# A gated mix of linear attention and a gated MLP: block products for half of the down projection, stored weights, and scaled tokens

## The chip, the core and the metric

The kernel runs on one core of a Trainium2 chip. The metric is the device time of one execution in microseconds (us); lower is better. The engines are named as in the profile: PE is the matrix engine (PEld its weight loads), DVE the vector engine, ACT the scalar engine, POOL the GpSimd engine, and SP the engine that only issues the DMAs here. Matrix products read SBUF and write PSUM, which has eight banks of 128 rows by 512 columns of f32.

## The reference

```python
S, D, H, F = 2048, 576, 32, 4608          # tokens, model width, heads, hidden width
g = sigmoid((x * gate_w).sum(-1, keepdims=True))     # one gate per token
a = linear_attention(x, wqkv, w_phi) @ wo            # softmax feature maps, 32 heads of 18
gate, up = x @ W_gate, x @ W_up                      # [S, F] each
h = gate * (gate > 0) * up
b = h @ W_down                                       # [S, D]
out = g * a + (1 - g) * b
```

Everything is f32. The kernel gets near f32 precision from products in fp32r: each operand is split into a high part (its rounding to fp32r, made by ACT as a copy) and a low part (what is left, made by DVE as a subtraction), and each product is three matmuls, high by high, high by low and low by high.

## The kernel before

All arrays are kept transposed: features lie on the partitions, tokens on the free axis, 512 tokens to a block.

**Attention, first part** (to about 260 us in the profile): keys, values and queries of the 16 blocks of 128 tokens, one after another (loop over `t`). POOL multiplies half of each softmax. The gate's logit is a column of the values' product; `gate_logits` (L258) turns it into exp(-logit), and after the loop two small DVE instructions make g.

**Attention, second part** (to about 417 us): for each block of 512 tokens `sums`, `invert`, `divide` and `project_out`. g * a goes to the DRAM buffer `att` (L557). `gates` (L504, L505) spreads 1-g of each token over all 128 partitions, into `ngb`. The operands of the MLP are made in the same stretch by `x_operands` (L564 loads, L569 to L571 split, four subtractions on DVE between them).

**MLP** (the rest): `units` are the 2 halves of the tokens times 36 chunks of 128 hidden features. For gate and up the kernel multiplies 2x2 blocks (features halved by tokens halved) with 7 products instead of 8: `product(ps, u, n)` (L720) is product `n` of unit `u`, 7 matmuls of 128x128 by 128x512 each. Its weights are split in each unit anew, in both halves of the tokens: `load_w` (L601) brings 768 KB, `split_blocks` makes the operand tile `wb`, `split_sums` four sums of blocks (L621 to L624) and the operand tile `ws` (L604 on ACT, L607 and L608 on DVE). The seven operands `xo` of the tokens are exchanged between the halves, in the last unit of the first half (`prep`, from `x_operands(1)`).

The hidden blocks are split into `hh` and `hl`. The down projection runs one group of two chunks behind, in pieces between the products, for each row block `m` of the output and token block `t`:

```python
            for u in us:
                hh, hl = HID[u, t]
                w = WD[u][:, m * P:(m + 1) * P]
                pairs += [(w, hh), (w, hl)]
                if m < 4:
                    pairs.append((WD[u][:, DK + m * P:DK + (m + 1) * P], hh))
```

That is 8 x 6 matmuls for the four full row blocks and 2 x 4 for the fifth, which carries the high and the low part of its 64 rows side by side: 56 for a group of two units, with 2 x 49 of the products beside them. Two of the ten sums stay in PSUM over the whole half (`pm`); the other eight are added to `ac` in SBUF by DVE after each group (L770). After the last group of a half, `finish` loads `att` (L733), multiplies by `ngb` (L740), adds (L741) and stores (L742), for each of the ten blocks.

The order on each engine comes from a planner that goes by priorities in program order, except inside `in_order`, which pins the order as written on DVE, ACT and SP for the early operands. Buffers are rings: a tile waits until its predecessor in the ring has been read.

Of the kernel before, what the change touches and what calls it, by code (L numbers as in the profile page):

```python
# [47 lines left out]
@contextmanager  # L48
def in_order(tc, nc):

    traced = nc.cur_bb.bb.instructions
    last = {i.engine: i for i in traced}
    n = len(traced)
    yield
    for i in traced[n:]:
        if i.engine in (nc.vector.engine, nc.scalar.engine, nc.sync.engine):
# [6 lines left out]
def gated_mix_kernel(  # L63
# [33 lines left out]
    ngb = keep.tile([P, S], F32, name="ngb")  # L97
# [3 lines left out]
    gs = keep.tile([P, 4 * NT], F32, name="gs")[:, :NT]  # L101
# [158 lines left out]

    def queries(t):
# [81 lines left out]

    for t in range(2, NT - 1):
        if t in (6, 10):
            load_x(t // 4 + 1)
        if t == 12:
            AR.close()
# [44 lines left out]
    nc.vector.tensor_scalar_add(gs, gs, 1.0)  # L393
    nc.vector.reciprocal(gs, gs)
# [56 lines left out]
    rx = ctx.enter_context(tc.tile_pool(name="rx", bufs=1, **L_))  # L451
# [107 lines left out]

    def x_operands(hf):  # L560

        def load(k, t, slot):
            a = rx.tile([P, 3, TB], F32, name=f"xr{slot}")
            nc.sync.dma_start(a, xs[:, k, :, (2 * hf + t) * TB:(2 * hf + t + 1) * TB])  # L564
            return a

        def operand(name, a):
            o = (xo2 if name in (3, 4) else xo).tile([P, 5, TB], F32R, name="xo", tag="xo")
            nc.scalar.activation(o[:, 0:3], a, AF.Copy)  # L569
            tt(out=o[:, 3:5], in0=a[:, 0:2], in1=o[:, 0:2].bitcast(F32), op=SUB)  # L570
            tt(out=o[32:64, 2], in0=a[32:64, 2], in1=o[32:64, 2].bitcast(F32), op=SUB)  # L571
            XO[hf, name] = o

        b11, b12, b22 = load(0, 0, 0), load(0, 1, 1), load(1, 1, 2)
        operand(1, b11)
        yield
        tt(out=b11, in0=b12, in1=b11, op=SUB)
        operand(5, b11)
        yield
        tt(out=b11, in0=b22, in1=b11, op=SUB)  # L580
        operand(6, b11)
        yield
        tt(out=b12, in0=b22, in1=b12, op=SUB)
        operand(7, b12)
        b21 = load(1, 0, 1)
        yield
        operand(2, b21)
        yield
        operand(3, b22)
        yield  # L590
        tt(out=b21, in0=b21, in1=b11, op=SUB)
        operand(4, b21)
        yield
# [4 lines left out]
    def load_w(u):  # L598
        if u < len(units):
# [3 lines left out]
    def split_w(o, a, after=None):  # L603
        i = nc.scalar.activation(o[:, :, 0:3], a, AF.Copy)  # L604
        if after:
            tc.add_manual_dep(i.ins, after.ins.name, NO_SYNC, reason="after")
        tt(out=o[:, :, 3:5], in0=a[:, :, 0:2], in1=o[:, :, 0:2].bitcast(F32), op=SUB)  # L607
        tt(out=o[64:96, :, 2], in0=a[64:96, :, 2], in1=o[64:96, :, 2].bitcast(F32), op=SUB)  # L608

    def split_blocks(u, after=None):  # L610

        if u < len(units):
            o = wop.tile([P, 3, 5, P], F32R, name="wb")
            split_w(o, RAW[u][:, 0:3], after)
            WO[u] = {1: (o, 0), 2: (o, 1), 4: (o, 2)}

    def split_sums(u):

        if u < len(units):
            a = RAW.pop(u)  # L620
            tt(out=a[:, 2], in0=a[:, 2], in1=a[:, 3], op=ADD)  # L621
            tt(out=a[:, 3], in0=a[:, 0], in1=a[:, 3], op=SUB)
            tt(out=a[:, 0], in0=a[:, 2], in1=a[:, 0], op=SUB)
            tt(out=a[:, 1], in0=a[:, 1], in1=a[:, 0], op=SUB)  # L624
            o = wop.tile([P, 4, 5, P], F32R, name="ws")
            split_w(o, a)
            WO[u].update({5: (o, 2), 6: (o, 0), 7: (o, 3), 3: (o, 1)})

# [4 lines left out]
    early = x_operands(0)  # L633

    def later():
        with in_order(tc, nc):
            next(early)

    behind = iter(())
    for n, tb in enumerate(order):  # L640
# [50 lines left out]
    wdp = ctx.enter_context(tc.tile_pool(name="wdp", reuse_waits="tile", bufs=2))  # L691
    hp = ctx.enter_context(tc.tile_pool(name="hp", reuse_waits="tile", bufs=7))
    tp = ctx.enter_context(tc.tile_pool(name="tp", reuse_waits="tile", bufs=5))
    ac = ctx.enter_context(tc.tile_pool(name="ac", reuse_waits="tile", bufs=1))
    px = ctx.enter_context(tc.tile_pool(name="px", bufs=2, space=PSUM, reuse_waits="tile"))
# [81 lines left out]
    def step():  # L777
        next(behind, None)
# [142 lines left out]
```

## Time and profile before

| What | Value |
|---|---|
| Median of 3 runs | 1705.72 us (1703.13 to 1708.34) |
| The profiled execution | 1707.41 us |
| Its span in the profile | 1705.6 us |
| Granted PE clock, mean | 0.98 |
| PE busy | 1648.6 us, 7834 matmuls |
| DVE, ACT, POOL busy | 1291.1, 624.0 and 46.0 us |
| DMA | 128.48 MB, mean 75 GB/s |

The span is what the profile records from the first to the last instruction; the execution's own time has 1.8 us around it. A matmul's record ends later than the next one starts, since they are pipelined, so how many start in a stretch says more than how long each is. A row of a table by stretches gives the stretch, its length, then for each engine the busy time and the number of instructions (x), then the granted clock, the share of time in which the 16 DMA engines were busy, and GB/s.

### The profile page before, as it was taken

The numbers are of one execution on the slowest core, as the hardware profiler recorded it, in microseconds if no ns is written. First come the engines' busy times: TensorE is split into PE (matmuls) and PEld (weight loads), VectorE is DVE, ScalarE is ACT, GpSimd is POOL, SyncE is SP. The second block draws the span as 40 slices with busy tenths as digits, with TensorE's granted clock in tenths as the row PEclk, the third lists the DMA queues.
The fourth block names the chain that finished last, engine by engine and source line by source line (L and its number), as shares of the span: only waits on it lengthen the run. The fifth ranks groups of instructions, "written<-read, shape, count | busy, mean of one in ns | idle before, by whom it ended". The sixth has DMA issues, their size and how long they took to land.

```text
span 1705.6 us, 19899 instructions
## 1 busy us (share of the span) xinstructions
PE 1648.6 (97%) x7834; PEld 1379.0 (81%) x7834; DVE 1291.1 (76%) x1966; ACT 624.0 (37%) x895; POOL 46.0 (3%) x53
## 2 busy tenths in 40 slices
PE   9999997988999999999999998999999999999996
PEld 8899995666888888888888886788888888888885
DVE  5877675666778777777778779977777777777776
ACT  4233335554533333333323334433333332333330
POOL 0121210000000000000000000000000000000000
PEclk9899997889999999999999999999999999999998
DMA  5211113535221211122122212421111222121203
GB/s 182 69 37 58 44 44 96 170 127 169 83 70 65 70 51 60 61 65 70 51 70 66 70 51 70 149 83 62 63 61 52 70 65 70 51 70 60 63 18 105
DMA packets 42329, 128.48 MB, mean 75 GB/s; under 512 B 4906, under 2 KB 5546, under 8 KB 42236
## 3 DMA queue, kind: packets, MB, share of 16 engines
q1 hardware_dynamic: 42236, 127.22, 23.1%
q8 instruction: 61, 1.00, 0.2%
q14 instruction: 32, 0.26, 0.0%
HBM read 108.50 MB, written 16.74 MB: 73 GB/s over the span
## 4 chain that ended last, share of the span: by engine, by line
PE 86%; DVE 5%; DMA 4%; ACT 2%; issue 1%; SPq 1%; DVEq 0%; ACTq 0%
PE cx L720 26%; PE pd L763 19%; PE ca L720 13%; PE cy L720 6%; PE pm L763 5%; PE pq L150 4%; PE pk L150 3%; PE pv L150 3%; PE kv L319 2%; PE pwo L150 2%; PE ptr L283 1%; DMA ga<-att 1%; PE po L150 1%; DMA xr<-xs 1%; DMA wdr<-wd 1%
## 5 line engine op out<-in xcount | busy, mean ns | idle before, releaser
L763 PE MATMUL pd<-hh,wd 128*128 128x512 f32 x1008 | 357.5, 390 | 2.2 <-DVE ac L770 2.2
L720 PE MATMUL cx<-xo,ws 128*128 128x512 f32 x1008 | 253.2, 390 | 5.3 <-DVE ws L608 2.2
L720 PE MATMUL cx<-xo,wb 128*128 128x512 f32 x1008 | 252.5, 390 | 2.8 <-DVE o L556 1.4
L720 PE MATMUL ca<-xo,ws 128*128 128x512 f32 x1008 | 253.4, 390 | 0.8 <-DVE ws L608 0.6
L720 PEld LDWEIGHTS cx<-xo,ws 128*128 128x128 f32 x1008 | 188.8, 188 | 46.6 <-ACT g L789 2.7
L763 PE MATMUL pd<-hl,wd 128*128 128x512 f32 x576 | 224.6, 390 | 0.0
L720 PEld LDWEIGHTS cx<-xo,wb 128*128 128x128 f32 x1008 | 188.9, 188 | 43.8 <-DVE o L556 1.9
L763 PEld LDWEIGHTS pd<-hh,wd 128*128 128x128 f32 x1008 | 189.4, 188 | 43.1 <-DVE ac L770 3.5
L720 PEld LDWEIGHTS ca<-xo,ws 128*128 128x128 f32 x1008 | 189.2, 188 | 42.2 <-ACT wd L708 1.0
L770 DVE TENSOR_TENSOR ac<-pd,ac 128x512 f32<-128x512 f32 x272 | 187.5, 690 | 33.1 <-PE pd L763 33.1
L123 ACT ACTIVATE hh<-g 128x512 fp32r<-128x512 f32 x144 | 83.0, 621 | 294.3 <-DVE g L822 294.3
L708 ACT ACTIVATE wd<-wdr 128x576 fp32r<-128x576 f32 x72 | 48.8, 679 | 262.2 <-PE pd L763 256.0
L604 ACT ACTIVATE ws<-wr 128x1536 fp32r<-128x1536 f32 x72 | 107.3, 1490 | 59.5 <-DVE wr L624 59.5
L720 PE MATMUL cy<-xo,wb 128*128 128x512 f32 x504 | 126.6, 389 | 0.0
L763 PEld LDWEIGHTS pd<-hl,wd 128*128 128x128 f32 x576 | 108.4, 188 | 22.4
L607 DVE TENSOR_TENSOR ws<-wr,ws 128x1024 fp32r<-128x1024 f32 x72 | 88.2, 1225 | 44.1 <-ACT ws L604 43.9
L607 DVE TENSOR_TENSOR wb<-wr,wb 128x768 fp32r<-128x768 f32 x72 | 69.0, 958 | 55.1 <-ACT wb L604 53.5
L720 PEld LDWEIGHTS cy<-xo,wb 128*128 128x128 f32 x504 | 94.6, 188 | 19.6
L763 PE MATMUL pm<-hh,wd 128*128 128x512 f32 x288 | 101.0, 389 | 0.0
L800 ACT ACTIVATE g<-cx 128x512 f32<-128x512 f32 x72 | 43.1, 598 | 153.4 <-PE cx L720 147.4
L822 DVE SCALAR_TENSOR_TENSOR g<-g,cx 128x512 f32<-128x512 f32 x72 | 49.5, 687 | 60.2 <-PE cx L720 60.1
L815 DVE TENSOR_TENSOR g<-ca,g 128x512 f32<-128x512 f32 x72 | 49.8, 691 | 58.4 <-PE ca L720 58.3
(180 smaller groups left out, 2555.2 us busy)
## 6 DMA issues: line engine op xcount, KB each, us to landing
wr<-wgu SPq DMA_DIRECT2D x72, 768.0 KB
wdr<-wd SPq DMA_DIRECT2D x72, 288.0 KB
eT<-et SPq DMA_DIRECT2D x12, 594.0 KB
er<-eT SPq DMA_DIRECT2D x12, 594.0 KB
xr<-xs SPq DMA_DIRECT2D x8, 768.0 KB
att<-o SPq DMA_DIRECT2D x16, 256.0 KB
ga<-att SPq DMA_DIRECT2D x16, 256.0 KB
outT<-o SPq DMA_DIRECT2D x16, 256.0 KB
```

Of the source, the lines that this page charges most:

```text
L123: nc.scalar.activation(hi, src, AF.Copy)
L150: nc.tensor.matmul(ps, w, m, start=i == 0, stop=i == len(pairs) - 1)
L319: nc.tensor.matmul(kv[j // 2][:vn + 1, j % 2, :gn], v[:, j * GS:j * GS + vn + 1], flat(e)[:, c0:c0 + gn], start=False, stop=t == NT - 1, s ...
L604: i = nc.scalar.activation(o[:, :, 0:3], a, AF.Copy)
L607: tt(out=o[:, :, 3:5], in0=a[:, :, 0:2], in1=o[:, :, 0:2].bitcast(F32), op=SUB)
L708: nc.scalar.activation(o[:, :D], w, AF.Copy)
L720: nc.tensor.matmul(ps, w, v, start=first and m == 0, stop=m == len(pairs) - 1, skip_group_check=True)
L763: nc.tensor.matmul(ps, w, v, start=i == 0 and (g == 0 or not perm), stop=i == len(pairs) - 1 and (g == NGR - 1 or not perm))
L770: tt(out=ACC[m, t], in0=ps, in1=ACC[m, t], op=ADD)
L800: nc.scalar.activation(g2, cx, AF.Copy)
L815: tt(out=g2, in0=ca, in1=g2, op=ADD)
L822: nc.vector.scalar_tensor_tensor(out=g, in0=g, scalar=0.0, in1=up, op0=ALU.max, op1=MULT)
```

## The change

1. **Down projection, second half of the tokens**: each group of two chunks is treated as 2x2 blocks (two hidden chunks by two 128-row blocks of the output, with two token blocks) and multiplied with 7 products of 3 matmuls instead of 8 (`down`). The fifth row block still takes 8 matmuls, of the hidden blocks 1, 5, 2 and 4 of the seven. The hidden operands are seven sums instead of four blocks; the sums of weights are made by POOL (`down_sums_of_blocks`). The first half keeps its 56 matmuls a group (`down_plain`). The pieces are now one to a product, in `slot`: piece j of seven follows product j of the unit, in the order 1, 5, 6, 3, 7, 2, 4 of the block products, and DVE's addition of a piece is queued behind the product after it. Pieces 1, 6, 7, 4 add up in one PSUM bank, the others use a second.
2. **Gate and up weights**: the split operand tiles `wb` and `ws` of the first half are stored in DRAM (`wbd`, `wsd`, 0.98 and 1.31 MB a unit) and loaded in the second half instead of being made again (`load_operands`). In the first half unit u makes the weights of unit v = u + 1 (`make`). The units 0 and 1 are split before the MLP begins.
3. **Tokens times the root of 1-g**: the MLP's tokens are scaled beforehand, so that the hidden values carry 1-g and `finish` is gone: `ac` starts as `att`, loaded at the beginning of a half, and is stored as it is. The root needs g of half of the tokens early (`half_gates`, with an ACT square root), spread over the partitions (`on_all_rows`); POOL scales the tokens and makes the differences (`scaled_sums`), in the attention's first part for the first half and during the MLP's first half for the second. The seven operands go to DRAM (`xt`) and come back.
4. **Order**: the whole MLP is written in the order in which each of the five engines runs it (`in_order` over all of them). The exchange of the token operands is spread over the last unit of the first half and the first of the second (`swap_in`).

```diff
+    def half_gates(hf):
+        c = slice(hf * NT // 2, (hf + 1) * NT // 2)
+        nc.vector.tensor_scalar_add(gs[:, c], gs[:, c], 1.0)
...
+        nc.scalar.activation(rs[:, c], ng[:, c], AF.Sqrt)
...
+    def scaled_sums(hf, b, sb, c0, n):
+        b11, b12, b21, b22 = b
+        pt = nc.gpsimd.tensor_tensor
+        put = lambda i, a: nc.sync.dma_start(xt[:, hf, i - 1, :, c0:c0 + n], a)
...
+        for i, a in enumerate(b):
+            pt(out=a, in0=a, in1=sb[:, i % 2, None, :].to_broadcast([P, 3, n]), op=MULT)
+            yield
+            if i != 1:
+                put((1, 0, 2, 3)[i], a)
+        for i, o, a, c in ((5, b11, b12, b11), (7, b12, b22, b12), (6, b22, b22, b11), (4, b21, b21, b22)):
+            pt(out=o, in0=a, in1=c, op=SUB)
+            yield
+            put(i, o)
...
+        if t == 8:
+            half_gates(0)
...
+            first_half = scaled_sums(0, [xw.tile([P, 3, TB], F32, name="xb") for _ in range(4)], sb, 0, TB)
+        for _ in range(3):
+            next(first_half, None)
...
-    nc.vector.tensor_scalar_add(gs, gs, 1.0)
-    nc.vector.reciprocal(gs, gs)
+    half_gates(1)
...
+    def load_operands(u):
+        c = units[u][1]
+        b, o = wop.tile([P, 3, 5, P], F32R, name="wb"), wop.tile([P, 4, 5, P], F32R, name="ws")
+        nc.sync.dma_start(b.bitcast(F32), wbd[c])
+        nc.sync.dma_start(o.bitcast(F32), wsd[c])
...
+    def down_sums_of_blocks(g, m):
+        a = down_raw(g, m)
+        pt(out=a[:, 2], in0=a[:, 2], in1=a[:, 3], op=ADD)
...
+    def load_acc(hf, i, m, t):
+        a = ACC[hf, i, m, t] = ac.tile([P, TB], F32, name=f"ac{i}{m}{t}")
+        nc.sync.dma_start(a, att[rows(i, m, t, hf)])
...
+    def down(g, s, bank):
+        hf, first, last = g // NG, g % NG == 0, g % NG == NG - 1
+        m, i = divmod(s, 7)
+        n = DOWN[i]
+        key = 0 if n in (1, 6, 7, 4) else 1
+        if n in (1, 5, 2):
+            BANK[m, key] = bank(m, n)
+        ps = BANK[m, key]
+        h, l = HID[g, n]
+        o, k = WD[g, m], PLACE[n]
...
+        mm(ps, o[:, 0, k], h, n in (1, 5, 2), False)
+        mm(ps, o[:, 0, k], l, False, False)
+        mm(ps, o[:, 1, k], h, False, True)
+        if m == 0 and n in (1, 5, 2, 4):
...
+            mm(REST[r], w, h, first and n in (1, 5), False)
+            mm(REST[r], w, l, False, last and n in (2, 4))
+        def add():
+            i, t = ADDS[n]
+            a = ACC[hf, i, m, t]
+            tt(out=a, in0=ps, in1=a, op=ADD)
+            return [(hf, i, m, t)] if last and LAST.get(n) == (i, t) else []
+        return add
+    def store(keys):
+        for hf, i, m, t in keys:
+            nc.sync.dma_start(out[rows(i, m, t, hf)], ACC.pop((hf, i, m, t)))
+            if hf == 0:
+                load_acc(1, i, m, t)
...
+        def slot(j, ps, n, first):
+            product(ps, u, n, first)
+            if PEND:
+                done.extend(PEND.pop()())
+            if g > 0:
+                q = g - 1
+                PEND.append(down_plain(q, 7 * odd + j) if q < NG else down(q, 7 * odd + j, one_bank))
+            store(done)
...
+            for f in work:
+                f()
...
+        slot(0, cx, 1, True)
+        if u == 1:
+            nc.sync.dma_start(wbd[u], WB.pop(u).bitcast(F32))
+        if make:
+            blocks(v, high_w)
+        elif NC - 1 <= u < 2 * NC - 1:
+            load_operands(v)
...
+        nc.scalar.activation(g1, cx, AF.Copy)
...
+        slot(2, cx, 6, False)
+        if make:
+            nc.sync.dma_start(wbd[v], WB.pop(v).bitcast(F32))
+            block_sums(v, high_w)
...
+        if 0 < u < NC - 2:
+            load_w(u + 2)
...
+        if u == 1:
+            for i in range(8):
+                load_acc(0, i // 2 % 2, i // 4, i % 2)
+            load_rest(0)
+        if make:
+            nc.sync.dma_start(wsd[v], WS.pop(v).bitcast(F32))
...
+            def second():
+                tt(out=r[0], in0=g2, in1=r[0], op=SUB)
+                tt(out=r[1], in0=g2, in1=r[1], op=SUB)
+                split_h((g, 6), r[0])
+                split_h((g, 2), g1)
+                tt(out=g1, in0=g1, in1=r[0], op=SUB)
...
+    with in_order(tc, nc, nc.tensor, nc.vector, nc.scalar, nc.gpsimd, nc.sync):
+        load_down(0)
+        load_w(2)
+        for u in range(len(units)):
+            chunk(u)
...
+        put(0, 0, 1)
+        carry(0)
+        add()
...
+        put(1, 5, 6)
+        add()
+        store_rest(1, 1)
+        store(work)
```

More of the change, by code (lines that the diff above doesn't have):

```diff
@@ L55, in in_order @@
     for i in traced[n:]:
[L56 removed]
+        if i.engine in [e.engine for e in engines]:
             if i.engine in last:
@@ L558, in project_out @@
             yield
-    def x_operands(hf):
[L562 to L593, printed above, removed]
+    SEQ = (1, 5, 6, 2, 7, 3, 4)
@@ L775, in gated_mix_kernel, with rows @@
-    behind = iter(())
-    def step():
-        next(behind, None)
-    for _ in early:
-        pass
-    for u, (hf, c) in enumerate(units):
-        last = hf == 0 and c == NC - 1
-        prep = x_operands(1) if last else iter(())
-        cx = px.tile([P, TB], F32, name="cx")
-        product(cx, u, 1, True)
-        next(prep, None)
-        g1 = tp.tile([P, TB], F32, name="g1", tag="tp")
-        first = nc.scalar.activation(g1, cx, AF.Copy)
-        ca = pa.tile([P, TB], F32, name="ca")
-        product(ca, u, 5, True)
-        next(prep, None)
+    def rows(i, m, t, hf):
+        r = (2 * i + m) * P
+        return slice(r, r + P), slice((2 * hf + t) * TB, (2 * hf + t + 1) * TB)
@@ L819, in gated_mix_kernel @@
-        for t, (g, up) in enumerate(((g1, cx), (g2, u2))):
-            hh = hp.tile([P, TB], F32R, name="hh")
-            hl = hp.tile([P, TB], F32R, name="hl")
-            nc.vector.scalar_tensor_tensor(out=g, in0=g, scalar=0.0, in1=up, op0=ALU.max, op1=MULT)
-            split(hh, hl, g)
-            HID[u, t] = hh, hl
-        step()
-        WO.pop(u)
-        if c % DG == DG - 1:
-            for _ in behind:
-                pass
-            behind = down(hf, c // DG)
-    for _ in behind:
-        pass
+        if odd and plain and g > 0:
+            plain_down(g, high)
+        elif odd and g > 0:
+            down_blocks(g, 0, high)
+            down_blocks(g, 0, low)
+            rest_weights(g, 0)
+            rest_weights(g, 1)
@@ new lines, in chunk @@
+        if units[u] == (1, 1):
+            rest_rows(0, 0)
+        swap_in(u, 2)
+        if u == 0:
+            next(early, None)
+        cy = py.tile([P, TB], F32, name="cy")
+        slot(3, cy, 2, True)
+        if odd and plain and g > 0:
+            plain_down(g, low)
+        elif odd and g > 0:
+            down_sums_of_blocks(g, 0)
+        tt(out=g1, in0=cy, in1=g1, op=ADD)
+        swap_in(u, 3)
+        if u == 0:
+            plain_down(0, high)
+        slot(4, cx, 7, False)
@@ new lines, in chunk @@
+        if make:
+            block_sums(v, low_w)
+            block_sums(v, low_w_rows)
+        if 0 < u < NC - 2:
+            load_w(u + 2)
+        if odd and not plain:
+            down_block_sums(g, 0, high)
+            rest_weights(g, 2)
+        tt(out=u2, in0=cx, in1=u2, op=ADD)
+        if units[u] == (1, 1):
+            rest_rows(0, 1)
+        swap_in(u, 4)
+        slot(5, ca, 3, False)
+        if odd and not plain:
+            down_block_sums(g, 0, low)
+            rest_weights(g, 3)
@@ new lines, in chunk @@
+        tt(out=g2, in0=ca, in1=g2, op=ADD)
+        nc.vector.scalar_tensor_tensor(out=g2, in0=g2, scalar=0.0, in1=u2, op0=ALU.max, op1=MULT)
+        if plain:
+            high_h((g, odd, 1), g2)
+        elif odd:
+            high_h((g, 3), g2)
+        swap_in(u, 5)
+        if u == 0:
+            plain_down(0, low)
+        slot(6, cx, 4, False)
+        if u == 0:
+            nc.sync.dma_start(wbd[u], WB.pop(u).bitcast(F32))
+            nc.sync.dma_start(wsd[u], WS.pop(u).bitcast(F32))
@@ new lines, in chunk @@
+        if u == 1:
+            for i in range(8):
+                load_acc(0, i // 2 % 2, i // 4, i % 2)
+            load_rest(0)
+        if make:
+            nc.sync.dma_start(wsd[v], WS.pop(v).bitcast(F32))
+        if plain:
+            low_h((g, odd, 1), g2)
+        elif odd:
+            r = RH[g]
+            low_h((g, 3), g2)
+        if not odd and g > 0:
+            load_down(g)
+        nc.vector.scalar_tensor_tensor(out=g1, in0=g1, scalar=0.0, in1=cx, op0=ALU.max, op1=MULT)
+        swap_in(u, 6)
```

462 lines of the change are left out of this document (343 added, 119 removed).

## The prediction

> **What bounds the kernel now.** I read the page from the top: busy shares, slices, the chain that ended last; then the groups by line, stretches of time, and PE's waits.
>
> ```profile
> PE 1648.6 (97%) x7834; PEld 1379.0 (81%) x7834; DVE 1291.1 (76%) x1966; ACT 624.0 (37%) x895; POOL 46.0 (3%) x53
> ...
> PE   9999997988999999999999998999999999999996
> ...
> PE 86%; DVE 5%; DMA 4%; ACT 2%; issue 1%; SPq 1%; DVEq 0%; ACTq 0%
> ```
>
> PE is the bound: 97% busy, 86% of the chain. The places that are not full are slices 7, 9 and 10 (the attention's second part), 25 (the change of halves) and the last. By stretches:
>
> ```profile
> 600.00:700.00 100.00, 100.00 (x443) 82.84 (x442) 78.18 (x121) 34.60 (x47) 0.00 (x0) 1.00 0.19 62
> ...
> 1000.00:1100.00 100.00, 92.64 (x387) 72.15 (x386) 91.85 (x136) 43.33 (x54) 0.00 (x0) 0.98 0.34 105
> ...
> 1100.00:1200.00 100.00, 100.00 (x440) 82.10 (x439) 80.53 (x126) 38.58 (x52) 0.00 (x0) 1.00 0.20 66
> ...
> 417.00:445.00 28.00, 26.00 (x112) 20.78 (x113) 21.68 (x38) 13.01 (x19) 0.00 (x0) 1.00 0.44 131
> ...
> 1680.00:1706.00 26.00, 10.27 (x44) 7.66 (x42) 18.38 (x29) 1.26 (x2) 0.00 (x0) 0.77 0.56 161
> ```
>
> In the steady MLP 443 matmuls start in 100 us: 0.2257 us each, no wait, full clock. A unit of 77 (49 products, 28 of the down projection) takes 17.4 us; DVE has 78% of that. The change of halves starts 387 instead of 443: 56 x 0.2257 = 12.6 us lost, with DVE 92% busy. The MLP's first 28 us start 112 instead of 124: 2.7 us lost.
>
> **Part 1, the down projection.** Its matmuls now:
>
> ```profile
> L763 PE MATMUL pd<-hh,wd 128*128 128x512 f32 x1008 | 357.5, 390 | 2.2 <-DVE ac L770 2.2
> ...
> L763 PE MATMUL pd<-hl,wd 128*128 128x512 f32 x576 | 224.6, 390 | 0.0
> ...
> L763 PE MATMUL pm<-hh,wd 128*128 128x512 f32 x288 | 101.0, 389 | 0.0
> ...
> L763 PE MATMUL pm<-hl,wd 128*128 128x512 f32 x144 | 56.1, 390 | 0.1
> ```
>
> Together 2016 = 36 groups x 56. In the second half a group becomes 14 x 3 + 8 = 50, six fewer. For 17 of the 18 groups (the last is in the tail, below) that is 102 x 0.2257 = **23.0 us less**, if PE stays the bound. What must hide beside it is DVE:
>
> ```profile
> L770 DVE TENSOR_TENSOR ac<-pd,ac 128x512 f32<-128x512 f32 x272 | 187.5, 690 | 33.1 <-PE pd L763 33.1
> ...
> L607 DVE TENSOR_TENSOR ws<-wr,ws 128x1024 fp32r<-128x1024 f32 x72 | 88.2, 1225 | 44.1 <-ACT ws L604 43.9
> ...
> L607 DVE TENSOR_TENSOR wb<-wr,wb 128x768 fp32r<-128x768 f32 x72 | 69.0, 958 | 55.1 <-ACT wb L604 53.5
> ...
> L608 DVE TENSOR_TENSOR ws<-wr,ws 32x512 fp32r<-32x512 f32 x72 | 49.2, 683 | 1.0
> ...
> L621 DVE TENSOR_TENSOR wr<-wr 128x384 f32<-128x384 f32 x72 | 40.2, 558 | 2.3
> ```
>
> In a group of the second half DVE has 14 additions (8 before), 10 instructions of the gate and up results, 4 differences and 7 low parts of hidden blocks: 35 x 0.69 = 24.2 us. Low parts of the down weights: two of 384 and two of 512 columns, 2 x 0.56 + 2 x 0.69 = 2.5, and two of the fifth row block, at most 0.56 each. Sum 27.8 us of 98 + 50 = 148 x 0.2257 = 33.4: 83%. That fits because the weight splits go (per unit 1.23 + 0.96 + 0.68, a second row like L608, and four like L621). Where it is tight: piece 4 of one unit and piece 1 of the next use the same bank, with only product 1 (7 x 0.2257 = 1.6 us) between them, and DVE's addition must fall into that time, behind the multiplication of gate by up and, in odd units, a low part. I count 0.2 us of slack there, which I take as enough; if not, that is a rival.
>
> In the first half the count of matmuls, additions and splits per unit stays; cost nothing, hidden as now (78%).
>
> **Part 3, the tail.** Last product, last vector instruction, and the transfers that the chain passes:
>
> ```profile
> 1674.31 1.75 PE L720 MATMUL cx<-xo,wb 128*128 128x512 f32 x7
> ...
> 1683.45 3.90 DMA ga<-att
> ...
> 1693.04 3.26 DMA ga<-att
> ...
> 1697.49 3.93 DMA ga<-att
> ...
> 1701.52 0.68 DVE o L741
> ```
>
> From the end of the last product (1676.1) to the end of the span (1705.6) it is 29.5 us, of which three loads of `att`, 256 or 128 KB, are 11 us; they are issued late, behind stores in SP's queue. After the change no load is left there, but one group's 14 pieces alternate with 14 additions, and DVE has some 27 instructions of 0.69 us: 18.6 us, about 3 of waiting for PE, 3.4 for the last store (as now from 1702.2): 25 us. **4.5 less**; ends 0 and 8.
>
> **Part 2, the stored weights.** Per unit of the first half the DMA moves 0.79 MB in for gate and up, 0.29 for down, and now 2.29 out: 3.37 MB in 17.4 us, 194 GB/s. In the second half 2.29 + 0.29 in 16.7 us: 155 GB/s. What the queues can do:
>
> ```profile
> 320.00:340.00 20.00, 18.62 (x85) 14.43 (x83) 10.24 (x16) 11.21 (x18) 0.00 (x0) 1.00 0.79 252
> ...
> 1040.00:1045.00 5.00, 4.25 (x12) 3.04 (x13) 4.94 (x7) 1.63 (x2) 0.00 (x0) 0.71 0.87 295
> ...
> 130.00:135.00 5.00, 5.00 (x39) 4.88 (x38) 3.24 (x6) 1.77 (x2) 1.16 (x1) 1.00 0.18 69
> ```
>
> 252 GB/s over 20 us, loads and stores mixed, and 295 over 5; the third stretch holds only stores of `eT`, and its share per GB/s is no higher, so stores cost no more than loads. I reckon with 295; 0.26 MB are 0.9 us by that, and a load of `att` took 3.3 to 3.9, so a transfer takes some 2.5 us more to land. Steady state: cost nothing, hidden behind PE. At the start it isn't. Units 0 and 1 have no down projection, so they last only 98 x 0.2257 = 22.1 us, and the queue holds down weights 0.59, weights of unit 2 0.79, four stores of units 0 and 1 4.59, `wb` of unit 2 0.98, weights of unit 3 0.79: 7.7 MB, 26 us, and 2.5 to land. Unit 3's weights then come at about 29 us, where ACT wants them at 24 (in unit 2, ahead of the copy that product 6 waits for, 4.5 us into the unit): PE waits some 1.5 us there, and the same a unit later, since `ac`'s 2.4 MB follow. With 2 us of DVE as now: 5 lost against 2.7, **+2.3**. Ends: -2.7, and +12 if those 2.4 MB and `ws` of unit 2 (1.3 MB), 12.5 us together, delay in full.
>
> **Part 4, the change of halves.** Weight splits end there on DVE (none in unit 35 or later), and `finish` goes. PE's waits now:
>
> ```profile
> PE cx L720 <- DVE ws L608: 2.2, 1, 2.2
> ...
> PE pd L763 <- DVE ac L770: 1.7, 1, 1.7
> ...
> PE cx L720 <- ACT g L789: 1.3, 1, 1.3
> ```
>
> All come from DVE and ACT being crowded with operands, splits and `finish`; that crowd leaves. Late next is the DMA: from the start of unit 35, 1.31 (`ws` of 35) + 2.29 (weights of 36) + 5 x 0.79 (operands) = 7.5 MB, 25.5 us, while the split of the last operand is queued on ACT about 22 us and on DVE about 25 us after it. DVE stands perhaps 4 us there, with additions of the down projection behind it. SP also waits for each of the eight stores of `ac` before it may load the next `att` into the same buffer, about 4 us each over two units, ahead of the next weights. I take 4 us lost instead of 12.6: **8.6 less**; ends 0 and 12.6.
>
> **Part 3, earlier.** In the attention's first part POOL gets 8 instructions of 1536 columns, DVE and ACT small ones, ACT a root:
>
> ```profile
> L182 POOL TENSOR_TENSOR e<-e,sm 128x576 f32<-128x576 f32 x16 | 24.3, 1521 | 87.4 <-DVE sm L244 87.4
> ...
> L182 POOL TENSOR_TENSOR e<-e,r 128x576 f32<-128x576 f32 x16 | 18.7, 1169 | 84.6 <-DVE r L269 79.1 <-PE kv L319 4.4 <-PE ptr L283 1.1
> ...
> L123 ACT ACT_TABLE_LOAD x1 | 1.3, 1283 | 0.7 <-PEq L913 0.7
> ...
> 100.00:200.00 100.00, 100.00 (x714) 94.48 (x712) 71.79 (x99) 35.77 (x57) 19.95 (x20) 1.00 0.14 48
> ...
> 260.00:280.00 20.00, 14.31 (x73) 10.30 (x72) 15.35 (x39) 13.16 (x28) 1.69 (x2) 0.77 0.36 110
> ```
>
> 8 x 1.169 x 1536/576 = 25 us of POOL, spread over four turns of 15 us, with PE full and POOL 20% busy: hidden, its results are wanted turns later. The root may need other tables than the exponential; the trace has one load of 1.28 us and no root, so 0 to 3 loads, 0 to 3.9 us of ACT, of which only the last stands where PE has gaps already (260 to 280 us). In the second part four subtractions leave DVE, the split of unit 1 (about 6 us of DVE) and three more loads of 0.79 MB come. I take **+2** for all of it, ends -3 and +6; and **+1** for POOL's 16 instructions of 768 columns in the MLP.
>
> By the Trainium skill (ScalarE: Activation LUTs, What ACT_TABLE_LOAD costs) a switch costs 2.66 us with its drain, and exponential and root lie in different sets; by it the three switches are an estimated 8 us of ACT, and the last one alone would put 1.4 us on the sum. The trace agrees on the 1283 ns and can't show the rest.
>
> **Sum.** -23.0 + 2.3 - 8.6 - 4.5 + 2 + 1 = -30.8. The profiled execution took 1707.4, so 1676.6; it lies 1.7 above the median of the runs, so 1675.
>
> **Rivals.** *All smooth*: no loss at the start, none at the change of halves, tail 21.5. -23.0 - 12.6 - 8 - 2.7 = -46, so 1660. For it: DMA has slack in every steady stretch. Against: 25 us of transfers in 17 us units.
>
> *PE waits for DVE in the second half*: the bank above is free half a microsecond too late in each of 36 units. +18, so 1693. For it: 83% with in-order queues; against: today's 78% gives no wait at all. POOL's 8 sums of weights a group, 8 x 1.169 x 128/576 = 2.1 us, can also hold up DVE; the two rows of POOL above differ by 0.35 us for the same work, the slower beside a DVE instruction. By the Trainium skill (SBUF — State Buffer, Who interferes with whom) a GpSimd instruction that reads SBUF and a DVE instruction with two SBUF inputs shut each other out for the whole instruction; 0.35 us is less than that.
>
> *The first half becomes bound by DMA* (the slower side): stores and loads together stay under the needed rate. It turns slower than before from 17.4 + 30.8/34 = 18.3 us a unit, 3.37 MB in that: below 184 GB/s. At 170 GB/s a unit takes 19.8 us, +84 in 34 units, so 1759. Against it stands the row with 252 GB/s.
>
> *The gain is eaten*: the six matmuls turn into waits of the same length and start and change of halves lose 12 us more: about 1705.
>
> **How the numbers follow.** Forecast 0.55, all smooth 0.15, PE waits 0.19, eaten 0.05, DMA-bound 0.06. The range 1660 to 1695 leaves out half of the smooth case and the last two. 0.3% is about 5 us, what a measurement of this kernel can tell from no change: faster 0.90, same 0.03, slower 0.07, with the eaten case shared out over the three.
>
> **What would show it.** 50 matmuls in a group of the second half and 443 starts in 100 us there; DVE about 83%; about 195 and 155 GB/s in the halves; no load of `att` after the last product; under 5 us lost between units 35 and 38. Wrong it would be by waits of PE for DVE's `ac` in each unit, or for `wb` and `ws` from DRAM.

## The result

The changed kernel takes 1685.9 us (median; 1685.6 to 1687.1) against 1707.0 for the kernel before in the same runs: a ratio of 0.988 (95% interval 0.986 to 0.990), 21 us or 1.2% faster. Run a second time it took 1684.9, ratio 0.9873 (0.9857 to 0.9890). The profiled execution has a span of 1683.8 us, 21.8 less than before. The forecast of 1675 had the sign and lies 11 us too low.

The page of the changed kernel, busy times, PE's slices and shares of the chain:

```profile
PE 1624.7 (96%) x7726; PEld 1357.8 (81%) x7726; DVE 1256.9 (75%) x1881; ACT 592.3 (35%) x962; POOL 213.8 (13%) x257
...
PE   8999998798999999999999999999999999999997
...
PE 65%; DVE 6%; DMA 2%; ACT 2%; issue 1%; SPq 0%; ACTq 0%; DVEq 0%
```

PE is still the bound, with 108 matmuls less. The slices that are not full are 1, 7, 8 and 10 (the attention part) and the last; 25 is full now, and none is new in the MLP. But a 9 stands for anything from 90%, so the stretches are needed:

```profile
417.00:445.00 28.00, 24.49 (x97) 19.08 (x98) 17.77 (x25) 10.93 (x15) 0.00 (x0) 0.94 0.99 360
500.00:600.00 100.00, 95.83 (x420) 78.19 (x418) 82.74 (x111) 33.45 (x46) 16.92 (x8) 1.00 0.57 202
600.00:700.00 100.00, 97.97 (x430) 80.71 (x431) 78.42 (x111) 32.31 (x45) 8.18 (x4) 1.00 0.64 227
1000.00:1100.00 100.00, 96.64 (x417) 78.92 (x416) 72.56 (x101) 37.50 (x59) 17.03 (x14) 0.98 0.65 232
1200.00:1300.00 100.00, 100.00 (x443) 82.69 (x442) 75.93 (x123) 30.04 (x60) 12.55 (x27) 1.00 0.42 156
1658.00:1684.00 26.00, 16.91 (x69) 12.05 (x67) 20.48 (x34) 5.18 (x9) 5.95 (x7) 0.95 0.26 91
```

Columns as before: PE, PEld, DVE, ACT and POOL busy, granted clock, DMA share, GB/s. The second half (1200 to 1300) runs as forecast: 443 matmuls, no gap, DVE 76%. The first half does not: 420 and 430 starts where before had 443, in the two stretches where POOL is busy (16.9 and 8.2 us). PE's waits name what it stood for (us in total, how many, the longest):

```profile
PE cx L874 <- ACT g L1080: 11.7, 8, 2.0
PE chain L914 <- DVE ac L920: 3.4, 2, 1.9
```

Stage by stage, from the starts of each unit's first product in the traces (us; the kernel before was profiled three times, the changed one twice; the end of a product is taken as 0.23 us after its last matmul starts):

| kernel | first product | units 0, 1 | units 2 to 33 | units 34 to 39 | units 40 to 71 | end of last product to end |
|---|---|---|---|---|---|---|
| before | 417.1 / 417.1 / 420.4 | 24.9 / 24.0 / 24.0 | 558.5 in each | 117.8 / 117.5 / 117.2 | 557.6 in each | 29.7 / 30.1 / 30.1 |
| after | 417.1 / 412.4 | 28.3 / 29.7 | 569.7 / 569.8 | 109.7 / 110.2 | 536.6 / 536.5 | 22.4 / 22.4 |
| no POOL arithmetic | 410.4 | 28.0 | 558.5 | 111.0 | 536.5 | 23.0 |
| copy first | 412.5 | 29.2 | 565.3 | 110.5 | 536.4 | 22.4 |
| arithmetic on DVE | 413.0 | 30.0 | 558.5 | 109.6 | 536.4 | 23.0 |
| plain second half | 411.1 | 29.6 | 572.8 | 112.0 | 558.5 | 21.0 |
| weights made again | 410.4 | 28.2 | 568.4 | 127.7 | 642.7 | 22.3 |
| change of halves | 413.1 | 29.7 | 573.9 | 109.7 | 536.7 | 22.4 |
| arithmetic on DVE, and change of halves | 413.9 | 30.0 | 558.5 | 108.9 | 536.6 | 22.8 |
| POOL in pieces | 413.1 | 26.9 | 561.1 | 110.3 | 536.6 | 22.4 |
| five edits | 414.4 | 27.1 | 558.5 | 107.1 | 536.6 | 22.8 |

The column of units 2 to 33 holds what the forecast missed: +11.2 us, in a stretch that it costed at +1. Nearly all of it (11.0) lies in six units (5, 7, 10, 15, 17 and 20), each 1.7 to 1.9 us longer than its neighbours of the same parity.

### The profile page after: what moved, and what is told of

Read it like the earlier page. It is cut to its first block, busy times and chain, and to the rows that moved or that the text cites. A ratio compares the mean times of both kernels' runs of the same rounds, so it can differ in the third digit from the quotient of the medians.

```text
span 1683.8 us, 20063 instructions
## 1 busy us (share of the span) xinstructions
PE 1624.7 (96%) x7726; PEld 1357.8 (81%) x7726; DVE 1256.9 (75%) x1881; ACT 592.3 (35%) x962; POOL 213.8 (13%) x257
## 4 chain that ended last, share of the span: by engine, by line
PE 65%; DVE 6%; DMA 2%; ACT 2%; issue 1%; SPq 0%; ACTq 0%; DVEq 0%
PE cx L874 24%; PE ca L874 12%; PE cy L874 6%; PE chain L937 5%; PE other L914 5%; PE chain L914 5%; PE other L937 4%; PE pm L937 2%; PE pm L914 1%; DVE wb L680 1%; DVE wb L683 1%; DMA xt<-xb 1%; ACT wb L677 1%; DVE ac L952 1%; DVE wr L698 0%
## 5 line engine op out<-in xcount | busy, mean ns | idle before, releaser
L874 PEld LDWEIGHTS cx<-xo,ws 128*128 128x128 f32 x1008 | 188.6, 188 | 54.5 <-ACT g L1080 15.1
L986 DVE TENSOR_TENSOR hl<-g,hh 128x512 fp32r<-128x512 f32 x198 | 135.4, 691 | 37.2 <-ACT hh L981 32.1
L937 PE MATMUL chain<-hh,wd 128*128 128x512 f32 x280 | 109.4, 391 | 3.4 <-DVE ac L952 1.9
L840 DVE TENSOR_TENSOR wd<-wdr,wd 128x384 fp32r<-128x384 f32 (+1 forms) x108 | 71.9, 680 | 50.0 <-ACT wd L837 50.0
L952 DVE TENSOR_TENSOR ac<-chain,ac 128x512 f32<-128x512 f32 x140 | 96.3, 688 | 17.0 <-PE chain L937 17.0
L914 PE MATMUL chain<-hh,wd 128*128 128x512 f32 x288 | 100.8, 391 | 3.4 <-DVE ac L920 3.4
L914 PE MATMUL other<-hh,wd 128*128 128x512 f32 x288 | 100.4, 389 | 0.0
L837 ACT ACTIVATE wd<-wdr 128x384 fp32r<-128x384 f32 (+1 forms) x108 | 63.7, 607 | 84.3 <-POOL wdr L829 81.3
L677 ACT ACTIVATE ws<-wr 128x1536 fp32r<-128x1536 f32 x36 | 53.6, 1488 | 100.0 <-DVE wr L701 89.5
L952 DVE TENSOR_TENSOR ac<-other,ac 128x512 f32<-128x512 f32 x105 | 72.0, 685 | 16.1 <-PE other L937 16.0
L937 PE MATMUL other<-hh,wd 128*128 128x512 f32 x210 | 81.7, 389 | 0.0
L1114 DVE TENSOR_TENSOR u<-cx,u 128x512 f32<-128x512 f32 x72 | 49.8, 691 | 32.0 <-PE cx L874 31.0
L1100 DVE TENSOR_TENSOR g<-cy,g 128x512 f32<-128x512 f32 x72 | 49.4, 686 | 27.2 <-PE cy L874 26.3
```

The costliest lines, as they stand in the source:

```text
L837: nc.scalar.activation(o[:, 0], a, AF.Copy)
L840: tt(out=o[:, 1], in0=a, in1=o[:, 0].bitcast(F32), op=SUB)
L874: nc.tensor.matmul(ps, w, v, start=first and m == 0, stop=m == len(pairs) - 1, skip_group_check=True)
L914: nc.tensor.matmul(ps, w, v, start=k == 0 and (i < 2 or first), stop=k == len(mms) - 1 and (i < 2 or last), skip_group_check=True)
L937: mm = lambda ps, w, v, a, z: nc.tensor.matmul(ps, w, v, start=a, stop=z, skip_group_check=True)
L952: tt(out=a, in0=ps, in1=a, op=ADD)
```

## The experiments

**Where the 11 us come from.** The timeline of the changed kernel in unit 5 (start, duration, engine and line, what, and the idle time before with its releaser):

```profile
502.56 0.56 DVE L699 TENSOR_TENSOR wr<-wr 128x384 f32<-128x384 f32 x1
502.74 8.10 POOL L296 TENSOR_TENSOR xb<-xb,sbp 128x768 f32<-128x768 f32 x4 [91.86 <-ACT u L1070]
...
503.15 2.08 DVE L700 TENSOR_TENSOR wr<-wr 128x384 f32<-128x384 f32 x1
...
505.27 2.08 DVE L701 TENSOR_TENSOR wr<-wr 128x384 f32<-128x384 f32 x1
...
507.28 0.68 DVE L920 TENSOR_TENSOR ac<-other,ac 128x512 f32<-128x512 f32 x1
507.44 1.49 ACT L677 ACTIVATE ws<-wr 128x1536 fp32r<-128x1536 f32 x1 [4.80 <-DVE wr L701]
...
508.83 0.58 ACT L1080 ACTIVATE g<-cx 128x512 f32<-128x512 f32 x1
...
509.46 1.89 PE L874 MATMUL cx<-xo,ws 128*128 128x512 f32 x7 [1.56 <-ACT g L1080]
```

The program issues one POOL multiplication per unit, but nothing makes POOL wait for the unit: once the first may start it runs four, one behind the other, in 8.10 us. DVE's third and fourth sum of the weight blocks (128x384, two operands in SBUF) take 2.08 us beside it; the second, just before, took 0.56. The first of the two starts at 503.15; POOL's first instruction ends at 504.82 (its second starts at 504.78), and 0.41 us later DVE's ends (505.23). Of its 2.08 us it stood still for some 1.5, nearly the whole rest of POOL's instruction. The addition at 507.28, one of whose operands lies in PSUM, takes its usual 0.68 beside the same POOL instructions. Behind the sums ACT converts the weight sums, 3.0 us late; behind that, in ACT's queue, stands the copy that frees PE's bank; PE waits 1.56 us.

*No POOL arithmetic* leaves out the second half's scaling:

```
 for i, a in enumerate(b):
-    pt(out=a, in0=a, in1=sb..., op=MULT)
+    if hf == 0: pt(out=a, in0=a, in1=sb..., op=MULT)
...
-    pt(out=o, in0=a, in1=c, op=SUB)
+    if hf == 0: pt(out=o, in0=a, in1=c, op=SUB)
```

> Leaves out POOL's 16 multiplications and differences of 128x768 in units 5 to 20, so the tokens of the second half are not scaled; their loads and stores stay. Theory (POOL holds up DVE's weight sums, ACT's conversion of the sums starts late, the copy of g2 stands behind it and PE waits): the six units that are 1.7 to 1.9 us longer return to 18.36 or 16.55 us, 11.0 us in all, and the time is about 1675. Rival (the loads and stores of these blocks, or the queue that issues them, cost the 11 us): the six units stay long and the time stays at 1686.

1671.0 us, ratio to the kernel before 0.9795 (0.9779 to 0.9811). Units 2 to 33 take 558.5 again, to the tenth what they took before the change, with all the loads and stores still there:

```profile
500.00:600.00 100.00, 100.00 (x443) 82.84 (x442) 78.42 (x116) 33.07 (x46) 0.00 (x0) 1.00 0.58 206
```

443 starts, DMA share as before it. The rival (the transfers) is out. The rest of the 14.9 us against 1685.9 is, in the profiles, mostly the earlier first product (below).

*Arithmetic on DVE* does the same work on another engine (`pt = nc.gpsimd.tensor_tensor if hf == 0 else tt`).

> The same 16 multiplications and differences on DVE, one at the end of a unit, instead of POOL. Theory (the instructions cost time only through the stretching of DVE's own beside POOL's): 16 of about 1 us each, in a half where DVE has a third of its time free, cost nothing; 1675 as without them. Rival (any work of this size at these places makes DVE late): each of the 16 units loses up to 1 us, 1686 to 1692.

1672.3 us, 0.9803 (0.9787 to 0.9820), units 2 to 33 at 558.5. So not the work and not its place in the unit cost time, but that POOL did it. The rows of the groups (busy us, mean ns of one, then the idle time before them), first the changed kernel's, then this one's:

```profile
L296 POOL TENSOR_TENSOR xb<-xb,sbp 128x768 f32<-128x768 f32 x8 | 16.3, 2064 | 179.1 <-ACT u L1070 91.9 <-DMA xb<-xs 87.3
```

```profile
L296 DVE TENSOR_TENSOR xb<-xb,sbp 128x768 f32<-128x768 f32 x8 | 7.6, 952 | 0.0
```

DVE needs 0.95 us for what POOL needs 2.06 for, and while POOL has it DVE can't do its own.

*POOL in pieces* asks whether DVE is shut out for a whole instruction or shares a rate: each instruction of 128x768 becomes four of 128x192.

```
-pt(out=a, in0=a, in1=sb[:, i % 2, None, :]..., op=MULT)
+for s in ([slice(0, n)] if hf == 0 else [slice(64 * k, 64 * k + 64) for k in range(n // 64)]):
+    pt(out=a[:, :, s], in0=a[:, :, s], in1=sb[:, i % 2, None, s]..., op=MULT)
```

> POOL does the same scaling of the second half's tokens, but each of the 16 instructions of 128x768 is cut into 4 of 128x192. Units 2 to 33 took 569.7 us with the whole instructions and 558.5 without POOL's arithmetic. Theory (a DVE instruction with two operands in SBUF cannot run until the POOL instruction under way has ended, and gets its turn between two): DVE's sums of 128x384 take at most one piece longer, about 1.1 us instead of 2.08, and units 2 to 33 take 558.5 to 563 us. Rival (the two share the rate at which SBUF is read for as long as POOL has work, whatever the size of its instructions): the sums still take about 2 us, and units 2 to 33 about 570 us.

1672.8 us, 0.9812 (0.9792 to 0.9831); units 2 to 33 take 561.1. Its timeline at the same place (lines three higher):

```profile
497.30 12.37 POOL L298 TENSOR_TENSOR xb<-xb,sbp 128x192 f32<-128x192 f32 x16 [91.61 <-ACT u L1073]
...
497.78 0.84 DVE L703 TENSOR_TENSOR wr<-wr 128x384 f32<-128x384 f32 x1
...
498.65 0.84 DVE L704 TENSOR_TENSOR wr<-wr 128x384 f32<-128x384 f32 x1
```

POOL is now busy longer, 12.37 us instead of 8.10, yet DVE's sums take 0.84 instead of 2.08: each waits for one piece (0.77 us on average) at most and runs before the next. Of the 11.2 us, 2.6 remain. The exclusion goes by the instruction; the rival (a shared rate) is out. So it is not the burst that hurts but the length of each instruction in it.

*Copy first* takes away what stands behind the late sums:

```
+g2 = tp.tile(...); nc.scalar.activation(g2, cx, AF.Copy)
 if make:
     block_sums(v, high_w)
-g2 = tp.tile(...); nc.scalar.activation(g2, cx, AF.Copy)
```

> ACT's copy of the finished second product (g2) is put ahead of its conversion of the weight sums in every unit that makes weights. Theory (the copy is late only because it stands behind the conversion, which waits for DVE's sums): PE no longer waits for the copy, in the six units beside POOL's bursts (1.7 to 1.9 us each) or in unit 1 (1.98 us); up to 13 us less, about 1673 to 1676. Rival (DVE itself is 3 us behind in these units, so that its additions come late whatever ACT does): PE waits for DVE's u or ac in the same units, and the time stays within 3 us of 1686.

1679.1 us, 0.9840 (0.9820 to 0.9859): a part of each theory. Waits of PE between 480 and 830 us, in the changed kernel and then in this one:

```profile
PE cx L874 <- ACT g L1080: 9.2, 6, 1.6
```

```profile
PE cx L874 <- DVE u L1115: 4.5, 4, 1.7
PE chain L914 <- DVE ac L920: 0.6, 1, 0.6
```

The copy no longer waits, but DVE has lost its 3 us all the same, and PE now stands for DVE's addition into u. Of the 11.2 us, 6.8 remain, unevenly: nothing in units 10 and 20, 1.0 to 1.1 us in 7 and 17, but 2.0 and 2.5 in 5 and 15, no less than before. In those two the late DVE costs as much as the late copy did. In unit 1, where the copy stood behind the same conversion, the 14.6 us become 14.1, for the same reason.

**What each half of the change is worth.** *Plain second half* keeps the stored weights but multiplies 56 matmuls a group in both halves (`plain = True`, accumulators by half, and a plain last group).

> The second half keeps its weights from DRAM, and its down projection is the plain one of the first half, 56 matmuls a group instead of 50. Theory (matmuls are the second half's price, and nothing else in it waits): a pair of units goes from 33.58 to 34.90 us, 17 x 1.32 = 22.4 us more, and the last group's end is some 1 to 5 us longer: 1709 to 1713. Rival (part of the gain comes from DVE and ACT not making the gate and up weights): the pair stays below 34.5 us and the time below 1702.

1706.8 us in one run. The units 40 to 71 take 558.5, 34.90 a pair, 21.9 more than the changed kernel. The first product of this run started 6.0 earlier than in the changed kernel's first profile, and one POOL burst cost 3 us more; hence 1706.8 and not 1709. Its second half:

```profile
1200.00:1300.00 100.00, 100.00 (x442) 82.78 (x442) 47.46 (x70) 19.95 (x33) 0.00 (x0) 1.00 0.37 143
```

DVE is down to 47% and ACT to 20%, and PE is no faster for it: keeping the weights alone gains nothing.

*Weights made again* is the other half alone: 50 matmuls, and the gate and up weights split in both halves.

```
-make = 0 < u < NC - 1
+make = 0 < u < 2 * NC - 1
-elif NC - 1 <= u < 2 * NC - 1: load_operands(v)
-if 0 < u < NC - 2: load_w(u + 2)
+if 0 < u < 2 * NC - 2: load_w(u + 2)
```

(and no stores of the kept weights)

> The 50 matmuls a group stay in the second half, but gate and up weights are made again in both halves from their raw blocks, and nothing is kept in DRAM. DVE then has in a group of the second half its 25.3 us (75.5% of 33.58) and the weights' some 11 us, 36 to 37 us, ACT some 16 us. Theory (DVE becomes the bound; keeping the weights is what makes the 50 matmuls worth their 22 us): a pair of units takes 36 to 38 us, 40 to 75 us more in all: 1725 to 1760. Rival (DVE's work is hidden still): 33.6 to 34.2 us a pair, 1686 to 1697.

1801.7 us in one run, 116 more than the changed kernel and 42 beyond the upper end of what was expected. A window of its second half, and PE's waits there:

```profile
1200.00:1300.00 100.00, 90.30 (x370) 70.06 (x368) 89.02 (x142) 36.14 (x60) 14.34 (x23) 0.97 0.15 52
```

```profile
PE other L937 <- DVE ac L952: 3.5, 2, 1.8
PE cx L874 <- DVE u L1107: 2.4, 3, 0.8
PE chain L937 <- DVE ac L952: 2.3, 2, 1.2
```

Most pairs of units take 40.7 us (40.2 on average). DVE's own work was sized rightly: 89% of 40.7 is 36.2 us. But PE and DVE wait for each other in turns, so the pair costs 4.5 us more than either has to do (PE 33.6, DVE 36.2). POOL's sums of down weights now run beside DVE's weight sums and stretch some of those from 0.55 to 0.70 us; by the durations this is an estimated 0.7 us of DVE in a pair. What the rest owes to POOL was not separated. The kept weights are what lets the 50 matmuls pay.

**The change of halves.** It lost 13.1 us before (117.8 against 6 x 17.45) and loses 6.3 now (109.7 against 103.4: twice 18.36 + 16.55 and once 17.71 + 15.87, as such pairs take without a wait). The trace shows there a wait of ACT for the down weights, whose load stands in SP's queue behind stores and loads that wait for one another:

```profile
1067.10 0.82 SPq L958 DMA_DIRECT2D outT<-ac  x1
...
1070.66 0.32 SPq L882 DMA_DIRECT2D ac<-att  x1
...
1071.08 0.38 SPq L958 DMA_DIRECT2D outT<-ac  x1
...
1074.60 0.32 SPq L882 DMA_DIRECT2D ac<-att  x1
...
1074.97 0.43 SPq L807 DMA_DIRECT2D wdr<-wd  x1
...
1080.14 0.53 ACT L837 ACTIVATE wd<-wdr 128x384 fp32r<-128x384 f32 x1 [3.07 <-DMA wdr<-wd]
```

Each load of `att` may go only when the store from the same buffer has landed, some 3.5 us later, and the load of the down weights follows the last of them. *Change of halves* moves it ahead and gives the rests of the operands to DVE:

```
-    low_rest(1, i - 5, pt)
+    low_rest(1, i - 5, tt)
...
+if u == NC - 1: load_down(NG)
...
-if not odd and g > 0: load_down(g)
+if not odd and g > 0 and g != NG: load_down(g)
```

> Only the edits of the change of halves: SP issues the load of group 18's down weights in unit 35 instead of behind the stores in unit 36, and the five 32x512 rests run on DVE instead of POOL. Units 34 to 39 took 109.7 us against 103.4 without a wait. Theory (ACT's wait for the down weights and DVE's operands stretched to 4.56 us by POOL are what is lost): the loss of 6.3 us falls to 1 to 3 us. Rival (DVE has too much to do in these units, whoever does the rests): it stays at 5 to 8 us.

1686.9 us, 0.9886 (0.9870 to 0.9902): nothing gained, units 34 to 39 again 109.7. (Its units 2 to 33 take 573.9 us because one POOL burst, in unit 5, cost 4.3 us more than in the changed kernel.) The waits of PE there, in the changed kernel and in this one:

```profile
PE chain L914 <- DVE ac L920: 3.4, 2, 1.9
```

```profile
PE cx L874 <- DMA wb<-wbd: 1.6, 1, 1.6
PE chain L914 <- DVE ac L920: 1.4, 1, 1.4
PE cx L874 <- DVE xo L638: 0.8, 1, 0.8
```

The first theory falls: the waits for DVE shrink from 3.4 to 2.2 us (1.4 and 0.8), and others take their place, the longest for the stored weights from DRAM, whose loads stand behind the same pairs in SP's queue. Together with the arithmetic on DVE it gave no more than that alone:

> Two edits together: the scaling of the second half's tokens on DVE, and at the change of halves the down weights of group 18 loaded in unit 35, ahead of the 8 pairs of stores and loads, and the rests of the new operands on DVE instead of POOL. If they are independent: the MLP is 11 us shorter for the first and 2 to 5 us for the second, about 1668 to 1670; if the extra work makes DVE late at the change of halves, no better than the first alone (1672).

1673.1 us, 0.9813 (0.9795 to 0.9830), against 1672.3; units 34 to 39 take 108.9 against 109.6.

**The better kernel.** *Five edits* adds to these the SP queue and the start:

```
 nc.sync.dma_start(out[rows(i, m, t, hf)], ACC.pop((hf, i, m, t)))
-if hf == 0: load_acc(1, i, m, t)
+while LATER: load_acc(*LATER.pop(0))
+if hf == 0: LATER.append((1, i, m, t))
...
-if units[u] == (1, 1): load_rest(1)
+if units[u] == (1, 3): load_rest(1)
...
 swap_in(u, 1)
-if u == 0: next(early, None)
...
-block_sums(v, high_w)
+if u > 1: block_sums(v, high_w)
 nc.scalar.activation(g2, cx, AF.Copy)
+if u == 1: block_sums(v, high_w)
```

> Meant as the better kernel: the scaling of the second half's tokens on DVE; at the change of halves the down weights loaded in unit 35, the load into each accumulator issued one store later, the loads of the last 64 rows in unit 39, the rests on DVE; at the start the last operand made after the copy of g2 in unit 0, and in unit 1 the copy of g2 ahead of the weight sums. Each wait is its own: units 2 to 33 in 558.5 us as with the first edit alone, units 34 to 39 in 106 to 108 instead of 109.6, units 0 and 1 in 27 to 28.5 instead of 30.0; 1667 to 1670 against 1672.3. If DVE's queue is what holds these units, the waits only move to its results, and the time stays at 1672 to 1673.

1668.7 us (1666.5 to 1670.9), 0.9789 of the kernel before (0.9769 to 0.9809), the fastest of all here and some 16 to 17 us below the changed kernel. Most of it is the arithmetic on DVE; units 34 to 39 take 107.1, and unit 1 13.5 instead of 14.6 to 14.9. (Unit 0 scatters from 12.3 to 15.1 us between kernels that have the same instructions there, with a granted clock of 1.00 up to 13.6 us and of 0.88 to 0.89 above; nothing is read from its 13.6.) The waits on DRAM are gone from the change of halves; DVE's stay, and with them 3.7 of the 6.3 us lost there:

```profile
PE chain L914 <- DVE ac L920: 1.4, 1, 1.4
PE cx L874 <- DVE xo L638: 0.8, 1, 0.8
```

**How much of it is the attention part.** The same instructions up to the first product started it at 417.1 in one kernel and at 410.4 in another, so the changed kernel and the one before were profiled again.

> The changed kernel once more, word for word, beside the next three on the same chip: in the four kernels run so far the first product starts at 410.4 to 413.0 us instead of 417.1, although their instructions up to there are the same. If that part only varies from run to run, this run starts somewhere between 410 and 417 us, its MLP takes 1266.7 us as before, and its time is 1680 to 1687. If the edits moved it, it starts at 417 again, and the time is 1686.

> The kernel before once more, with a profile. The first product of the changed kernel started at 417.1 us in one profile and at 412.4 in the next, with the same instructions. If the attention part of the kernel before varies as much, its first product starts between 410 and 417 us and its MLP takes the 1288.5 us of the first profile; if it is at 417 again, the change made the attention part up to 5 us shorter.

> The kernel before a third time, with a profile, for the start of its first product: 417.1 us in two profiles, where kernels with the changed attention part started at 410.4 to 417.1. Between 416 and 418 again: the attention part of the change is some 4 us shorter in most of its runs. Below 415: the part varies in both kernels, and nothing is to be read from it.

The rows of the first product: the changed kernel's two profiles, then the third of the kernel before:

```profile
417.06 2.19 PE L874 MATMUL cx<-xo,wb 128*128 128x512 f32 x7 [1.83 <-DVE o L610]
```

```profile
412.36 1.88 PE L874 MATMUL cx<-xo,wb 128*128 128x512 f32 x7 [1.79 <-DVE o L610]
```

```profile
420.42 0.96 PE L720 MATMUL cx<-xo,wb 128*128 128x512 f32 x3 [1.45 <-DVE o L556]
```

The first product starts at 410.4 to 417.1 us over the eleven profiles with the changed attention part (median 413.0), and at 417.1, 417.1 and 420.4 before. The 420.4 lies outside both cases that were expected, so the part varies in the kernel before too. Where it varies can be seen, for PE starts 2290 matmuls before the first product in all fourteen profiles:

| stretch | before (3 profiles) | after and variants (11) |
|---|---|---|
| span's start to the 501st matmul | 80.1 to 83.0 | 78.3 to 82.9 |
| 501st to 1701st (most of the rest of the first part) | 168.7 to 168.9 | 170.6 to 170.8 |
| 1701st to the first product | 167.8 to 168.5 | 160.4 to 163.8 |

The first 80 us scatter alike in both kernels. The granted clock scatters in them too: between 40 and 60 us it is 0.74 in all three profiles of the kernel before, 0.74 and 0.83 in the two of the changed kernel, 0.91 in the two that start at 410.4. From there on the change made the attention part shorter in each profile, by 2.2 to 6.4 us: 4.0 to 8.1 less in the second part, 1.7 to 2.0 more in the first. The first part's loss looks like the MLP's. POOL's eight instructions of 128x1536 run there almost without a break, from 134.8 to 165.9 us, and DVE's multiplications with two operands in SBUF stand beside them:

```profile
142.80 7.46 POOL L296 TENSOR_TENSOR xb<-xb,sb 128x1536 f32<-128x1536 f32 x2
```

```profile
143.57 3.36 DVE L186 TENSOR_TENSOR e<-e,sm 128x576 f32<-128x576 f32 x1
...
159.70 2.87 DVE L186 TENSOR_TENSOR e<-e,sm 128x576 f32<-128x576 f32 x1
```

In the turns before and after it the same multiplication takes 0.76 us. The loss falls on the 901st to the 1101st matmul (139 to 169 us): 30.0 us in each of the eleven profiles, against 28.1 to 28.2 before. No run took POOL's work out of this part, so this cause is read from the traces and not tested. By the medians of the timed runs the whole change is worth 20.3 and 21.1 us, about as much as the MLP's spans alone (18.7 to 21.8, from the first product to the end). The attention part's gain doesn't show there, and why stays open.

## Why the prediction was right, and where it was 11 us too low

Measured between the first profiles, beside the terms of the sum (the measured ones add up to the -21.8 us between the spans, within 0.1 of rounding):

- **The six matmuls**: -23.0 forecast, 17 x 1.32 = -22.4 measured. PE stayed the bound; DVE takes 76% and not 83%, mostly because its instructions of 0.69 us start 0.60 apart when they stand back to back (between 1200 and 1300 us the durations add up to 80.5 us, and DVE is busy for 75.9). That the bank between piece 4 and piece 1 had enough slack was right: not one wait of PE for `ac` from unit 40 to 70.
- **The start**: +2.3 forecast, +3.5 measured (+5.6 between the second profiles). The mechanism was wrong. The queue was as full as reckoned (360 GB/s in the first 28 us, well above the 295 I took), but the weights came in time, and unit 2 takes its usual 18.36 us. PE stands 2.5 us for ACT's copies and 0.9 for DVE's addition, and the granted clock is 0.52 between 419 and 422 us, 0.94 over the 28. The queue has a share in it by another way: in unit 0 ACT stands 2.1 us until a store of `att` has landed (1.0 in *POOL in pieces*), and the copy that PE wants comes after. *Five edits* gained 1.1 us in unit 1, 0.5 of which the copy's place alone gave in *copy first*.
- **The change of halves**: -8.6 forecast, -6.8 measured; 6.3 us lost instead of 4. SP's pairs of store and load, which the prediction named, are there with 3.5 us each.
- **The tail**: -4.5 forecast, -7.3 measured. DVE is busy 20.5 of the last 26 us; its instructions again start 0.60 apart, so 27 of them are 16 us and not 18.6.
- **Earlier**: +2 forecast, -0.1 measured in these profiles. Behind the small number stand three larger ones: +2.1 of scatter in the first 80 us, +1.8 where POOL's work was taken as hidden (25 us over four turns forecast, 28.8 us within two of them measured), and -4.0 in the second part.
- **POOL in the MLP**: +1 forecast, **+11.2** measured. This is the term that was mis-sized, by 10.2 us. Between the profiles the sum missed by 9.0 us; the rest of the 11 is the 1.7 us taken off for the median, which here lies 0.3 above the profiled execution.

With the last term as forecast, the sum would have come near the time: without POOL's arithmetic the kernel takes 1671.0, with it on DVE 1672.3. That is luck in part: the other five terms are off by 0.6 to 2.8 us each and nearly cancel. The step that failed is the term for POOL, which has no working beside it, and the sentence on POOL among the rivals that could have given it one. That sentence knew the rule that a GpSimd instruction and a DVE instruction with two operands in SBUF shut each other out for the whole instruction (the Trainium skill, SBUF — State Buffer, Who interferes with whom), set against it two rows of the kernel before that differ by 0.35 us, and let the rows decide. But those are means of POOL's own durations, over instructions beside which DVE did many things; the engine to look at was DVE, and with POOL instructions of 2 us beside it, which the kernel before did not have in the MLP. The rule should have been priced: a DVE instruction may stand for up to a whole POOL instruction, and two of them stand ahead of ACT's conversion. The runs here agree with the rule in each point that they touch: 0.56 us become 2.08 beside an instruction of 2.06; 0.68 stay 0.68 with an operand in PSUM; 0.84 beside pieces of 0.77.

The prediction also placed it in the wrong half. The second half has POOL work too, 8 sums of 128x128 a group:

```profile
L826 POOL TENSOR_TENSOR wdr<-wdr 128x128 f32<-128x128 f32 x36 | 16.7, 463 | 206.4 <-DVE wd L840 206.4
```

At such a length they hold DVE up too little to matter: between 1110 and 1650 us PE's waits show a single one, of 0.2 us, and not for DVE. In the first half the program has one instruction a unit, and an engine that nothing holds back doesn't keep such a schedule.

The other rivals: *all smooth* would have needed the start and the change of halves without loss, 12.4 us (28.3 against 98 x 0.2267 = 22.2, and 6.3); DMA did not bound the first half (units at 202 to 227 GB/s with PE full between the bursts); the gain was not eaten.

Of ACT's tables the forecast allowed up to three loads; the trace has four, at 126.6, 131.0, 255.3 and 259.6 us, each 1.28 us as before. Around the third of them stands nothing more:

```profile
254.14 1.17 ACT L179 ACTIVATE e<-e 128x1152 f32<-128x1152 f32 x1 [0.83 <-DVE e L178]
255.33 1.28 ACT L271 ACT_TABLE_LOAD   x1
256.62 0.21 ACT L271 ACTIVATE gates<-gates 128x8 f32<-128x8 f32 x1
```

From the end of the exponential (255.31) to the start of the root it is 1.31 us. So the 2.66 us for a switch with its drain, by the Trainium skill (ScalarE: Activation LUTs, What ACT_TABLE_LOAD costs), are not what this trace shows. Nor did PE pay at once for the first two loads: the 200 matmuls that start between 111 and 139 us take 28.1 us, and before the same ones took 28.2.

## What to carry to other kernels

Before work goes to POOL because it is idle, look at which DVE instructions with two SBUF operands will run beside it, and take each as stopped for the rest of POOL's instruction; what matters is then the longest POOL instruction and what is queued behind DVE, not POOL's share of the time. If DVE has time left (here it went from 78 to 82% busy), the work costs less there (0.95 us against 2.06); if it must be POOL, cut it into pieces of the size of DVE's own (that left 2.6 of the 11.2 us). And an order of one step a unit in the program is no schedule for an engine that waits for nothing.

## What the runs showed of the hardware

A single core's queues moved 389 GB/s at a DMA share of 1.01 between 420 and 440 us, with loads and stores mixed, and PE did not wait for them:

```profile
420.00:440.00 20.00, 17.47 (x72) 13.73 (x71) 12.89 (x19) 10.19 (x13) 0.00 (x0) 0.95 1.01 389
```

DVE's instructions of 128x512 last 0.68 to 0.69 us each but start 0.60 apart back to back (the two additions at 507.28 and 507.88), so a sum of durations overstates a crowded DVE by up to an eighth. And the 501st matmul starts at 78.3 to 82.9 us from profile to profile in eleven profiles of kernels that are alike up to there, while the 1200 matmuls from it on stay within 0.2 us: a difference between two programs is better read from a stretch than from the whole.
